# Fourier mixing and two gated layers: forward folds from GpSimd to VectorE, matrix loads ahead of folds, weight conversions at earlier steps

## The chip, the cores and the metric

The kernel runs on one core of a Trainium2 chip. The metric is the device time of one execution in microseconds (us), the median of three runs. The engines are named as in the profile: PE is TensorE (PEld its weight loads), DVE is VectorE, ACT is ScalarE, POOL is GpSimd, SP is SyncE, which only issues DMAs here.

## The reference

The input is 2 sequences of 3008 tokens with 256 features. Each is transformed along the tokens, mixed in the frequency domain by a complex 256x256 matrix with a bias, shrunk towards zero by 0.01 (soft threshold), and transformed back. The 6016 tokens then go through two gated layers of width 2048, whose weights come as 64-bit numbers; the second layer has exp(-h) in place of exp(-1.702 h).

```python
def _attn_ref(x, w_r, w_i, b_r, b_i):
    X = np.fft.rfft(x, axis=1)
    Xr, Xi = X.real, X.imag
    Yr = Xr @ w_r - Xi @ w_i + b_r
    Yi = Xr @ w_i + Xi @ w_r + b_i
    Yr = np.sign(Yr) * np.maximum(np.abs(Yr) - lam, 0.0)
    Yi = np.sign(Yi) * np.maximum(np.abs(Yi) - lam, 0.0)
    return np.fft.irfft(Y, n=x.shape[1], axis=1)

def _moe_ref(x, w_in, w_out):
    h = x @ w_in
    return (h * (1.0 / (1.0 + np.exp(-1.702 * h)))) @ w_out
```

## The kernel before

The kernel has four stages, one after another on PE.

**Forward transform** (from line 271, loop at line 458). The tokens are folded by symmetry: `fold(g)` (line 290) adds and subtracts quarter sequences on 128 partitions, so that a small matrix product does the transform. There are 16 groups, `groups`, in the order (frequency parity q, sequence b, kind t): groups 0 to 3 and 12 to 15 are q=0, groups 4 to 11 are q=1. A fold makes up to three tiles `lv` or `keep` (128x512, line 309), three tiles `xf` (128x256, line 320) and, for two kinds, two more `xf` from `dd` (line 329). The configuration strings `lv`, `dd` and `pr` say by position which engine does each: V is DVE, P is POOL. In group 2 and later, 9 operations stand on POOL: three `lv` or `keep`, four `xf` or their like at line 320 (in the groups with t=3, the ones with j=1, of which groups 13 and 15 are the last) and two at line 329. Step g of the loop issues the folds of group g+3, then `fwd_mm(g)` (line 366; matrix products at line 361), then for sequence 1 `load_m` (line 121, a DMA of a forward matrix at line 132 into one of four buffers `m0`), then `fwd_evac` of the group before (PSUM to `xt`, ACT at line 401, or ACT at line 405 and DVE at lines 391 to 417). `fold` also calls `load_raw` (line 284, a DMA at line 288 into one of three buffers). In this stage POOL and SP run in the written order; the order of DVE, ACT and PE is set at compile time by a planner with its own costs, and each engine then runs its list in that fixed order.

**Mixing** (from line 493, loop at line 567): 12 steps i of complex products (lines 518, 521), with the bias added by one product `ones` x `bias_hl` (line 524). Steps 0 and 1 use float32, the others a high and a low part `xh`, `xl`, with `wh` and `wl` (lines 502, 503). `bias_hl` is completed by a DMA on POOL (line 344). DVE and ACT threshold the result.

**Inverse transform** (from line 600): 16 steps, products at line 361 again (`psi`), evacuated by ACT and DVE, summed into `yt`, in part by accumulating DMAs on POOL (line 702).

**Two gated layers** (from line 771): per layer l, 6 blocks i of up to 1024 tokens, 8 pairs p of weight tiles. `group(l, i, p, hook)` (line 806) makes seven products (line 818) by a Strassen-like scheme, gates them on ACT (lines 821, 823), and the second products `out_mm` (line 790) follow one group later, so that group p's second weight is used in group p+1. ACT copies (lines 837, 853, 855) and DVE sums (lines 839, 863, 866) stand between the products. `hook(h)` is called at six places of a group, with h from 1 to 6. From the mixing on, every engine runs in the written order.

**Weight conversion** runs beside all this. The 32 weight tiles arrive as 64-bit numbers and become pairs of 32-bit parts. `cv_load` (line 154) loads one into `raw` (one buffer, SP, lines 162, 163, 166). `window(1, ())` (line 246) begins one conversion: `cv_bits` (line 169) has one ACT operation into `cv_c` (line 175; one buffer), then five DVE operations (lines 180 to 184) and an accumulating DMA on POOL from `cv_c` into `cv_a` (line 185), which are kept in a list that `pump` works off. `settle` hands finished ones on; `window(0, done)` places them: `place_out` (line 194: ACT at 105 and 107, a DMA on POOL at 106) or `place_in` (line 203: DVE at 213 to 216, ACT and POOL or DMAs). The order is that of `WEIGHTS` (line 33). The steps are lists in the configuration: `tf` in the forward stage (4 conversions), `tm` and `ml` in the mixing (3 conversions, and loads), `ti` in the inverse (3 conversions), `pl` in the inverse (placements), and `kb` for the 8 groups of the first block of tokens (6 conversions; at the place h=1 of the group). `pk` is how many items of the list are worked off in a step of the mixing (4).

Of the kernel before, what the change touches and what calls it, by code (L numbers as in the profile page):

```python
# [8 lines left out]

F32 = mybir.dt.float32  # L10
CFG = {'lv0': 'V', 'lv': 'VVVVVPVVVVVP', 'dd0': 'VPVVPPPPPVVP', 'dd': 'VVVVVVVVVVPV', 'ths': 'VVVVPV', 'thf': 'VVVP', 'ivf': 'V', 'cva': 'P', 'pol': 'PPPP', 'pil': 'P', 'mvl': 'PVVP', 'xl': 'V', 'xse': 'V', 'gl': 'VPPPPPPP', 'tf': [6, 9, 11, 14], 'tm': [1, 6, 10], 'ml': [4, 8], 'ti': [8, 11, 14], 'pl': [1, 4, 9, 12, 15], 'kb': [0, 1, 1, 1, 1, 1, 1, 0], 'kr': [0, 1, 0, 1, 0, 1, 1, 0], 'fa': 3, 'xp': [2, 4, 4, 5], 'xq': [1, 4, 1], 'xs': 4, 'xi': [7, 7, 9, 10, 10, 11, 8], 'xsi': 9, 'xo': (0, 1, 6, 2, 3, 4, 5), 'xd': (0, 1, 4, 6), 'ca': 4, 'tl': True, 'fwd': 'Pool,SP', 'rest0': 'all', 'rest1': 'all', 'last1': 'all', 'inv': 'all', 'mid': 'all', 'last0': 'all', 'thm': 'A', 'gl0': 'PVPVVVPV', 'gl2': 'PPPPPPPP', 'gl3': 'PPPPPPPV', 'xl0': 'V', 'xl1': 'V', 'pre': 14, 'pre2': 0, 'yd': 6, 'lvb': 6, 'mlp': 'all', 'pr': 'VVVP', 'pf': 'PV', 'eo': '0110', 'n32': 2, 'li': [8, 10, 11], 'lii': [0], 'xa': 4, 'nhb': 6, 'ddb': 6, 'mlp1': 'all', 'mlp2': 'all'}
NUM = dict(li=[5, 6, 7, 8], n32=2, pk=4, ydp=2, lii=[1, 3], xd=(), ml=[], pl=[], xo=range(7), pi=6, nhb=6, tf=[5, 9, 13], tm=[1, 3, 5, 7, 9, 11], ti=[0, 2, 4, 6, 8, 10, 12, 14, 14, 15, 15], kb=[2] * 8, kr=1, fa=3, fe=2, pm=0, nf=4, lvb=6, ddb=8, ivb=1, eob=1, fsb=6, f1=3, f2=0, fm=[7, 8, 9], fi=[1, 1, 2, 2], pre=13, pre2=1, yd=3, psh=0, ie=[12], xp=[1, 3, 4, 5], xq=[1, 2, 2], xs=5, nw=4, xi=[14, 14, 15, 15], xsi=13, rw=2, ca=4, cc=2, tb=1, tmn=1)

DEF = dict(pr="V", pf="V", lv0="V", lv="VPP", dd0="VVVVVP", dd="VPV", mpl="PV", ths="VP", thf="VVPP", fsl="VP", ivf="PPVV", cva="P", pol="P", pil="P", mvl="V", xl="PPVVPPP", xl0="PPVVPPP", xl1="PPVVPPP", xse="VP", gl="P", gl0="P", gl2="P", gl3="P", wcl="V", thc="V", thm="V")
# [7 lines left out]
P = 128  # L22
# [8 lines left out]
FS = 4  # L31

WEIGHTS = [("in", 0, p, True) for p in range(6)] + [("out", 0, p, True) for p in range(4)]
WEIGHTS += [(kind, 0, p, True) for kind, p in (("out", 4), ("out", 5), ("in", 6), ("in", 7), ("out", 6), ("out", 7))]
WEIGHTS += [(kind, 1, p, False) for kind in ("in", "out") for p in range(8)]

C_HI = float(np.uint32(0x0FEFFEF0).view(np.float32))
# [2 lines left out]
def split_sums(kind, q, p):  # L40
    return (kind, q) == ("f", 0) and CFG.get("eo", "1111")[p] == "1" or (kind, p) == ("i", 0) and CFG.get("eo", "1111")[2 + q] == "1"

# [14 lines left out]
def spectral_mlp_kernel(ctx, tc, xin, mfwd, minv, wc, bias, w_in1, w_out1, w_in2, w_out2, outT):  # L57
# [4 lines left out]
    def N(k):  # L62
        return CFG.get(k, NUM[k])

# [6 lines left out]
    def region(name):  # L71
        m = CFG.get(name, "none")
        if m == modes[-1] == "all":
# [161 lines left out]
    def settle(now=False):  # L235
        pump()
        for u, (a, c) in bits:
            if not u[3]:
                spilled[u[:3]] = d = dram_p.tile([P, 2 * CU], F32, name=f"w_{u[0]}{u[1]}_{u[2]}")
                nc.sync.dma_start(out=d, in_=a)  # L240
        fresh = [(u, a) for u, (a, _) in bits if u[3]]
        done, added[:] = (added + fresh, ()) if now else (added[:], fresh)
        bits[:] = []
        return done
# [36 lines left out]
    raws, lvs, xs = {}, {}, {}  # L281
# [174 lines left out]

    prev = None
    for g, (q, b, t) in enumerate(groups):
        fold(g + N('fa'))
        ps = fwd_mm(g)  # L460
        if b == B - 1 and m_order[0][0] == "f":
            load_m()
        if prev is not None:
            fwd_evac(*prev)
        prev = (g, ps)
        if g == 6:
            wc_p = opened("wc", "right")
            wc_s = m_p.tile([P, MW], F32, tag="m", name="wc_s")[:, : 6 * D].rearrange("p (k d) -> p k d", k=2)
            bias_hl = wc_p.tile([P, 2 * D], F32R, name="bias_hl")
            bias_lo = wc_p.tile([1, 2 * D], F32R, name="bias_lo")  # L470
            bias_f = wc_p.tile([P, 2 * D], F32, name="bias_f")
            nc.gpsimd.memset(bias_f, 0.0)
            ones = wc_p.tile([P, P], F32R, name="ones")
            ones_f = wc_p.tile([P, P], F32, name="ones_f")

            neglam = wc_p.tile([P, 1], F32, name='neglam')
            nc.vector.memset(neglam, -LAM)


        if g == 10:  # L480
            load_wc()
        if g == 13:
            prep_wc()
            lo_p.append(wc_p)
            xsplit(N('n32'), 1)
        if g == 3:
            cv_load(1)
        if g in N('tf'):
            tick(N('tf').count(g))
# [422 lines left out]
    done = []  # L912
    added.extend(hold)
    for at, (l, i, p) in enumerate(seq):
# [10 lines left out]
        def hook(h):  # L925
# [13 lines left out]
            if h == 3:  # L939
                window(0, done, True)  # L940
                done[:] = []
            if h == 1:
                window(k, ())
            if h in (2, 3):
                moved(h)
# [2 lines left out]
            if h == 4:  # L948
                pump()
                cv_load(1 - len(loaded))  # L950
            if late and (l, i, p, h) in ((0, 0, 1, 4), (0, 0, 2, 3), (0, 0, 2, 4), (0, 0, 3, 4)):
                kk, y, u, v = late.pop(0)
                (nc.vector.tensor_sub if kk in (0, 3) else nc.vector.tensor_add)(y, u, v)
# [152 lines left out]
```

## Time and profile before

| what | us |
|---|---|
| median of three runs | 1178.29 (1178.03 to 1184.57) |
| the profiled execution, its own time | 1182.72 |
| its span, first to last instruction | 1180.6 |
| PE busy | 1150.5 (97% of the span) |
| ACT / DVE / POOL busy | 773.3 / 636.1 / 502.4 |

The profile is of one execution. In its rows a time is the start in us from the begin of the span, followed by how long the merged instructions took, the engine, the line, the operation, the tiles and the count; in brackets is how long the engine had stood idle before and what ended that. Busy PE counts matrix products that are pipelined, so a product of 128x512 is shown with a longer time than the step to the next one.

### The profile page before, as it was taken

How to read it: one execution, taken by the hardware profiler on the slowest of the kernel's cores; microseconds unless marked ns; L12 is line 12 of the kernel's file. 1: busy time of each engine (PE TensorE's matmuls, PEld its weight loads, DVE VectorE, ACT ScalarE, POOL GpSimd, SP SyncE). 2: the span in 40 equal slices, each digit the busy share in tenths (PEclk: the TensorE clock that was granted, in tenths of full speed). 3: DMA queues.
4: the chain of work that ended last, by engine and by line, in shares of the span. 5: the costliest groups of instructions: out<-in, count | busy, mean ns of one | idle time of the engine just before them, and what ended most of it. 6: DMA issues, size and time to landing. Idle time of an engine off the chain costs nothing.

```text
span 1180.6 us, 14536 instructions
## 1 busy us (share of the span) xinstructions
PE 1150.5 (97%) x5052; PEld 945.3 (80%) x5052; DVE 636.1 (54%) x987; ACT 773.3 (65%) x1439; POOL 502.4 (43%) x430
## 2 busy tenths in 40 slices
PE   7889998999999999999999999999999999999998
PEld 4658885877888888888889978888888888888897
DVE  7768787776556466365564553352532623523522
ACT  2366545777668667667677787675665766766755
POOL 2355254443444444344446755433333433433333
PEclk9989999999999999999999999999999999999999
DMA  7457478432121221121130200010000000000000
GB/s 270 142 128 148 126 148 163 89 80 45 44 64 36 72 63 37 45 72 37 36 89 5 68 10 27 1 37 1 1 36 1 11 26 1 36 1 1 36 1 31
DMA packets 37835, 66.83 MB, mean 57 GB/s; under 512 B 3457, under 2 KB 14977, under 8 KB 37762
## 3 DMA queue, kind: packets, MB, share of 16 engines
q1 hardware_dynamic: 25730, 45.90, 11.9%
q0 software_dynamic: 12032, 20.01, 9.8%
q8 instruction: 39, 0.64, 0.2%
q14 instruction: 34, 0.28, 0.1%
HBM read 35.53 MB, written 10.35 MB: 39 GB/s over the span
## 4 chain that ended last, share of the span: by engine, by line
PE 76%; ACT 3%; DVE 2%; issue 1%; DMA 0%; DVEq 0%; POOL 0%; POOLq 0%
PE o L790 40%; PE x L818 36%; ACT yt L821 1%; DMA wo<-cv_a 0%; ACT x L727 0%; ACT yt L837 0%; DVE yt L839 0%; DVE tmp L213 0%; DVE yt L863 0%; ACT g L823 0%; DVE x L734 0%; ACT yt L855 0%; ACT yt L853 0%; DVE g L828 0%; DVE cv_a L182 0%
## 5 line engine op out<-in xcount | busy, mean ns | idle before, releaser
L828 POOL TENSOR_TENSOR g<-yt,g 128x512 fp32r<-128x512 f32 (+1 forms) x282 | 362.8, 1299 | 491.4 <-PE x L818 337.1
L790 PE MATMUL o<-g,wo 128*128 128x512 f32 (+1 forms) x2304 | 561.0, 386 | 2.6 <-DMA wo<-cv_a 2.6
L818 PE MATMUL x<-x,wi 128*128 128x512 f32 (+1 forms) x2016 | 501.2, 388 | 7.8 <-ACT yt L837 3.1
L790 PEld LDWEIGHTS o<-g,wo 128*128 128x128 f32 x2304 | 433.0, 188 | 83.8 <-DMA wo<-cv_a 3.1
L818 PEld LDWEIGHTS x<-x,wi 128*128 128x128 f32 x2016 | 378.2, 188 | 86.1 <-ACT yt L837 5.4
L821 ACT ACTIVATE yt<-yt 128x512 f32<-128x512 f32 (+1 forms) x288 | 179.1, 622 | 257.1 <-DVE yt L863 205.8
L823 ACT CAST g<-yt 128x512 fp32r<-128x512 f32 (+1 forms) x384 | 235.1, 612 | 12.2
L863 DVE TENSOR_TENSOR yt<-yt,x 128x512 f32<-128x512 f32 (+1 forms) x96 | 64.7, 674 | 217.2 <-PE x L818 216.7
L839 DVE TENSOR_TENSOR yt<-yt,x 128x512 f32<-128x512 f32 (+1 forms) x96 | 64.8, 675 | 167.4 <-ACT yt L837 167.4
L828 DVE TENSOR_TENSOR g<-yt,g 128x512 fp32r<-128x512 f32 (+1 forms) x102 | 70.1, 688 | 72.1 <-ACT g L823 72.1
L361 PE MATMUL psf<-m,xf 128*128 128x190 f32 (+3 forms) x224 | 57.7, 419 | 15.7 <-DVE xf L320 6.5
L361 PEld LDWEIGHTS psf<-m,xf 128*128 128x128 f32 x224 | 41.7, 204 | 31.1 <-POOL xf L320 7.9
L866 DVE TENSOR_TENSOR yt<-yt,x 128x512 f32<-128x512 f32 (+1 forms) x96 | 64.8, 675 | 0.0
L734 DVE TENSOR_TENSOR x<-yt,x 128x512 fp32r<-128x512 f32 (+1 forms) x44 | 46.1, 1047 | 29.7 <-ACT x L727 29.7
L185 POOL DMA_DIRECT2D cv_a<-cv_c x32 | 28.0, 875 | 77.5 <-DVE cv_c L184 61.4
L855 ACT COPY yt<-x 128x512 f32<-128x512 f32 (+1 forms) x96 | 55.8, 581 | 0.7 <-ACT yt L853 0.6
L821 ACT ACTIVATE yt<-x 128x512 f32<-128x512 f32 (+1 forms) x96 | 56.2, 585 | 0.0
L853 ACT COPY yt<-x 128x512 f32<-128x512 f32 (+1 forms) x96 | 55.0, 572 | 0.0
L837 ACT COPY yt<-x 128x512 f32<-128x512 f32 (+1 forms) x96 | 54.8, 571 | 0.0
L361 PE MATMUL psi<-m,f 128*128 128x376 f32 (+3 forms) x208 | 49.9, 396 | 0.0
L361 PEld LDWEIGHTS psi<-m,f 128*128 128x128 f32 x208 | 36.6, 190 | 11.9
L175 ACT ACTIVATE cv_c<-raw 128x512 f32<-128x512 f32 x32 | 21.6, 675 | 27.3 <-DMA cv_a<-cv_c 27.1
(117 smaller groups left out, 834.0 us busy)
## 6 DMA issues: line engine op xcount, KB each, us to landing
raw<-in_wi SPq DMA_DIRECT2D x32, 256.0 KB, 3.5
cv_a<-cv_c POOLq DMA_DIRECT2D x32, 256.0 KB, 5.0
raw<-in_wo SPq DMA_DIRECT2D x16, 512.0 KB, 4.0
raw<-in_x SPq DMA_DIRECT2D x12, 512.0 KB, 4.8
xl<-xt POOLq DMA_DIRECT2D x20, 256.0 KB, 5.5
out_t<-yt SPq DMA_DIRECT2D x20, 256.0 KB, 2.2
m<-in_mi SPq DMA_DIRECT2D x4, 564.0 KB, 9.1
wo<-cv_a POOLq DMA_DIRECT2D x8, 256.0 KB, 5.5
```

The source lines that it names most:

```text
L361: nc.tensor.matmul(ps, hi[:, c : c + P], m[:, k, :w], start=i == 0, stop=i == last)
L790: nc.tensor.matmul(acc[h, mm], st, mv, start=first and k == 0, stop=last and k == 2)
L818: nc.tensor.matmul(ps, st, mv, start=first and m == 0, stop=m == 2, skip_group_check=True)
L821: nc.scalar.activation(g, g if src is None else src, func)
L823: nc.scalar.copy(gh, g)
L828: eng.tensor_sub(gl, g, r32(gh))
L837: nc.scalar.copy(y1, X)
L839: nc.vector.tensor_add(y1, y1, Y)
L853: nc.scalar.copy(y2, Z)
L855: nc.scalar.copy(y3, X)
L863: nc.vector.tensor_add(y2, y2, X)
L866: nc.vector.tensor_add(y3, y3, Z)
```

## The change

- `lv`, `dd` and `pr` become 'V': all 9 fold operations of group 2 and later that stood on POOL go to DVE.
- In the loop of the forward stage, `load_m` stands before `fold`, and `fold` stands after `fwd_mm`.
- Mixing: conversions begin at steps 1, 5, 9 (were 1, 6, 10), loads at 3 and 7 (were 4 and 8), and 6 items of the list are worked off per step (were 4).
- Inverse: conversions begin at steps 5, 8, 11 (were 8, 11, 14); a sixth placement is added, at step 7.
- First block of tokens: conversions in groups 0 to 5 (were 1 to 6). In group 0 the conversion begins at h=4, its list is worked off at once and it is placed in group 1.
- The order of `WEIGHTS` has ("out", 6) before ("in", 6) and ("in", 7).

```diff
-CFG = {... 'lv': 'VVVVVPVVVVVP', 'dd': 'VVVVVVVVVVPV', 'pr': 'VVVP', 'tm': [1, 6, 10], 'ml': [4, 8], 'ti': [8, 11, 14], 'pl': [1, 4, 9, 12, 15], 'kb': [0, 1, 1, 1, 1, 1, 1, 0] ...}
+CFG = {... 'lv': 'V', 'dd': 'V', 'pr': 'V', 'tm': [1, 5, 9], 'ml': [3, 7], 'pk': 6, 'ti': [5, 8, 11], 'pl': [1, 4, 7, 9, 12, 15], 'kb': [1, 1, 1, 1, 1, 1, 0, 0] ...}
-WEIGHTS += [(kind, 0, p, True) for kind, p in (("out", 4), ("out", 5), ("in", 6), ("in", 7), ("out", 6), ("out", 7))]
+WEIGHTS += [(kind, 0, p, True) for kind, p in (("out", 4), ("out", 5), ("out", 6), ("in", 6), ("in", 7), ("out", 7))]
...
     for g, (q, b, t) in enumerate(groups):
-        fold(g + N('fa'))
         ps = fwd_mm(g)
         if b == B - 1 and m_order[0][0] == "f":
             load_m()
+        fold(g + N('fa'))
...
-            if h == 1:
+            if h == (1 if at else 4):
                 window(k, ())
...
             if h == 4:
                 pump()
                 cv_load(1 - len(loaded))
+                if at == 0:
+                    done.extend(settle(True))
```

## Rows read from the trace of the kernel before

**Rows 1.** The page: PE's busy time, and the granted TensorE clock in 40 slices
```profile
PE 1150.5 (97%) x5052; PEld 945.3 (80%) x5052; DVE 636.1 (54%) x987; ACT 773.3 (65%) x1439; POOL 502.4 (43%) x430
...
PEclk9989999999999999999999999999999999999999
```
**Rows 2.** The view of waits, engine PE, 0 to 300 us: total, times, longest
```profile
PE psf L361 <- POOL xf L320: 6.2, 3, 5.5
PE x L818 <- ACT yt L837: 3.0, 1, 3.0
PE psf L361 <- DMA m<-in_mf: 2.8, 1, 2.8
PE o L790 <- DMA wo<-cv_a: 2.6, 1, 2.6
```
**Rows 3.** The timeline of PE, from the forward transform into the mixing
```profile
28.52 2.20 PE L361 MATMUL psf<-m,xf 128*128 128x190 f32 x12 [0.49 <-DVE xf L320]
33.50 23.42 PE L361 MATMUL psf<-m,xf 128*128 128x376 f32 x98 [2.79 <-DMA m<-in_mf]
57.26 5.04 PE L361 MATMUL psf<-m,xf 128*128 128x188 f32 x30 [0.34 <-POOL xf L320]
...
68.61 4.75 PE L361 MATMUL psf<-m,xf 128*128 128x188 f32 x14 [5.49 <-POOL xf L320]
...
76.23 0.79 PE L524 MATMUL psm<-bias_hl,ones 128*128 128x512 f32 x1
```
**Rows 4.** The timelines of SP and of POOL in the forward transform
```profile
27.94 0.86 SPq L132 DMA_DIRECT2D m<-in_mf  x2
...
67.53 1.02 POOL L320 TENSOR_TENSOR xf<-keep 128x256 f32<-128x256 f32 x1
68.20 0.81 POOL L344 DMA_DIRECT2D bias_hl<-bias_lo  x1
```
**Rows 5.** The timeline of DVE at the end of the forward transform
```profile
65.93 0.69 DVE L184 SCALAR_TENSOR_TENSOR cv_c<-raw,cv_c 128x512 f32<-128x512 uint32 x1
...
67.14 0.40 DVE L320 TENSOR_TENSOR xf<-keep 128x256 f32<-128x256 f32 x1
```
**Rows 6.** The views of two tiles, DMA landing: bias_hl, then cv_c (to 300 us)
```profile
DMA to landing us min/median/max: 5.2/5.2/5.2
...
DMA to landing us min/median/max: 4.3/5.0/9.4
```
**Rows 7.** The timeline of PE, gated layers: where groups begin, and the second block
```profile
195.24 2.52 PE L818 MATMUL x<-x,wi 128*128 128x512 f32 x9
...
205.33 2.81 PE L818 MATMUL x<-x,wi 128*128 128x512 f32 x9 [0.38 <-DVE yt L863]
...
216.30 2.20 PE L818 MATMUL x<-x,wi 128*128 128x512 f32 x9
...
269.40 2.26 PE L818 MATMUL x<-x,wi 128*128 128x512 f32 x9
...
284.11 2.20 PE L818 MATMUL x<-x,wi 128*128 128x512 f32 x9
...
345.31 2.20 PE L818 MATMUL x<-x,wi 128*128 128x512 f32 x9
...
355.51 2.20 PE L818 MATMUL x<-x,wi 128*128 128x512 f32 x9
...
366.21 2.20 PE L818 MATMUL x<-x,wi 128*128 128x512 f32 x9
```
**Rows 8.** The timelines of ACT and POOL around the start of the gated layers
```profile
186.91 0.68 ACT L175 ACTIVATE cv_c<-raw 128x512 f32<-128x512 f32 x1 [3.31 <-DMA cv_a<-cv_c]
...
198.51 0.66 ACT L175 ACTIVATE cv_c<-raw 128x512 f32<-128x512 f32 x1 [5.49 <-DMA cv_a<-cv_c]
...
208.26 0.59 ACT L821 ACTIVATE yt<-x 128x512 f32<-128x512 f32 x1
...
202.30 0.86 POOL L185 DMA_DIRECT2D cv_a<-cv_c  x1 [8.03 <-DVE cv_c L184]
```

More of the change, by code (lines that the diff above doesn't have):

```diff
@@ L10 @@
 F32 = mybir.dt.float32
-CFG = {'lv0': 'V', 'lv': 'VVVVVPVVVVVP', 'dd0': 'VPVVPPPPPVVP', 'dd': 'VVVVVVVVVVPV', 'ths': 'VVVVPV', 'thf': 'VVVP', 'ivf': 'V', 'cva': 'P', 'pol': 'PPPP', 'pil': 'P', 'mvl': 'PVVP', 'xl': 'V', 'xse': 'V', 'gl': 'VPPPPPPP', 'tf': [6, 9, 11, 14], 'tm': [1, 6, 10], 'ml': [4, 8], 'ti': [8, 11, 14], 'pl': [1, 4, 9, 12, 15], 'kb': [0, 1, 1, 1, 1, 1, 1, 0], 'kr': [0, 1, 0, 1, 0, 1, 1, 0], 'fa': 3, 'xp': [2, 4, 4, 5], 'xq': [1, 4, 1], 'xs': 4, 'xi': [7, 7, 9, 10, 10, 11, 8], 'xsi': 9, 'xo': (0, 1, 6, 2, 3, 4, 5), 'xd': (0, 1, 4, 6), 'ca': 4, 'tl': True, 'fwd': 'Pool,SP', 'rest0': 'all', 'rest1': 'all', 'last1': 'all', 'inv': 'all', 'mid': 'all', 'last0': 'all', 'thm': 'A', 'gl0': 'PVPVVVPV', 'gl2': 'PPPPPPPP', 'gl3': 'PPPPPPPV', 'xl0': 'V', 'xl1': 'V', 'pre': 14, 'pre2': 0, 'yd': 6, 'lvb': 6, 'mlp': 'all', 'pr': 'VVVP', 'pf': 'PV', 'eo': '0110', 'n32': 2, 'li': [8, 10, 11], 'lii': [0], 'xa': 4, 'nhb': 6, 'ddb': 6, 'mlp1': 'all', 'mlp2': 'all'}
+CFG = {'lv0': 'V', 'lv': 'V', 'dd0': 'VPVVPPPPPVVP', 'dd': 'V', 'ths': 'VVVVPV', 'thf': 'VVVP', 'ivf': 'V', 'cva': 'P', 'pol': 'PPPP', 'pil': 'P', 'mvl': 'PVVP', 'xl': 'V', 'xse': 'V', 'gl': 'VPPPPPPP', 'tf': [6, 9, 11, 14], 'tm': [1, 5, 9], 'ml': [3, 7], 'pk': 6, 'ti': [5, 8, 11], 'pl': [1, 4, 7, 9, 12, 15], 'kb': [1, 1, 1, 1, 1, 1, 0, 0], 'kr': [0, 1, 0, 1, 0, 1, 1, 0], 'fa': 3, 'xp': [2, 4, 4, 5], 'xq': [1, 4, 1], 'xs': 4, 'xi': [7, 7, 9, 10, 10, 11, 8], 'xsi': 9, 'xo': (0, 1, 6, 2, 3, 4, 5), 'xd': (0, 1, 4, 6), 'ca': 4, 'tl': True, 'fwd': 'Pool,SP', 'rest0': 'all', 'rest1': 'all', 'last1': 'all', 'inv': 'all', 'mid': 'all', 'last0': 'all', 'thm': 'A', 'gl0': 'PVPVVVPV', 'gl2': 'PPPPPPPP', 'gl3': 'PPPPPPPV', 'xl0': 'V', 'xl1': 'V', 'pre': 14, 'pre2': 0, 'yd': 6, 'lvb': 6, 'mlp': 'all', 'pr': 'V', 'pf': 'PV', 'eo': '0110', 'n32': 2, 'li': [8, 10, 11], 'lii': [0], 'xa': 4, 'nhb': 6, 'ddb': 6, 'mlp1': 'all', 'mlp2': 'all'}
 NUM = dict(li=[5, 6, 7, 8], n32=2, pk=4, ydp=2, lii=[1, 3], xd=(), ml=[], pl=[], xo=range(7), pi=6, nhb=6, tf=[5, 9, 13], tm=[1, 3, 5, 7, 9, 11], ti=[0, 2, 4, 6, 8, 10, 12, 14, 14, 15, 15], kb=[2] * 8, kr=1, fa=3, fe=2, pm=0, nf=4, lvb=6, ddb=8, ivb=1, eob=1, fsb=6, f1=3, f2=0, fm=[7, 8, 9], fi=[1, 1, 2, 2], pre=13, pre2=1, yd=3, psh=0, ie=[12], xp=[1, 3, 4, 5], xq=[1, 2, 2], xs=5, nw=4, xi=[14, 14, 15, 15], xsi=13, rw=2, ca=4, cc=2, tb=1, tmn=1)
```

## The prediction, made before the changed kernel ran

> **What bounds the kernel now.** The page is read first. PE is busy for 1150.5 of 1180.6 us [rows 1], so at most 30 us are to be had from PE's gaps, and a little more from the clock: the granted clock falls to 8 tenths in one slice early on and to 9 in others [rows 1]. The other engines have room, so the share of busy time names PE, and the question is only where PE stands still. The view of waits of PE up to 300 us tells that [rows 2]: 6.2 us for folds on POOL, 2.8 for a forward matrix, 3.0 for an ACT copy at the start of the gated layers, 2.6 for a weight `wo` that is still in its DMA. From there on the groups begin at an even pace of 355.51 - 345.31 = 10.20 us, with 366.21 - 355.51 = 10.70 where one block of tokens follows another [rows 7], and nothing in the change touches that. So the sum is made of four places: the end of the forward transform, the mixing, the first two groups, and group 7 of the first block.
>
> **Forward transform.** Removed are three waits of PE: 2.79 at 33.50 for a matrix, 0.34 at 57.26 and 5.49 at 68.61 for a fold on POOL [rows 3]. The matrix is issued by SP at 27.94 [rows 4] because three loads of raw data stand before it in SP's queue and these wait for folds; after the change the first of the two matrices stands ahead of them and waits only for PE to leave its buffer, which is long done. Behind it SP then has the raw loads, which need folds that come later anyway, so I cost the move at nothing. A second matrix still follows the raw loads, with one group more of time. The folds: nine operations go to DVE, six of 128x256 at 0.40 and three of 128x512 at some 0.69 (taken from the nearest operation with two inputs of that size) [rows 5], 4.5 us of DVE time in 57 us; POOL took 1.02 for one [rows 4]. The one that PE waited for stood on POOL behind the DMA of the third conversion, which waits for DVE's last operation on it at 65.93 [rows 5]. In the changed kernel a fold needs nothing of the conversion, and the planner is free to put it earlier in DVE's list. I take it that it does, because there is nothing else in that list for DVE while a conversion's DMA is under way.
>
> What is late next? Without waits PE would start at 33.50 - 2.79 = 30.71, need 23.42 + 5.04 for the same products [rows 3], and 16 more of 5.04 / 30 = 0.168 each: it would end at 61.9 instead of 68.61 + 4.75 = 73.36. That is 11.5 us, of which 14 x (4.75 / 14 - 0.168) = 2.4 are the slow clock after the long wait. But the mixing cannot use all of it. Its product with `bias_hl` ran at 76.23 [rows 3]; the DMA for it was issued at 68.20 [rows 4] and takes 5.2 [rows 6], so it was there at 73.4, only 2.8 before its use. That DMA hangs on the same conversion (DVE at 65.93, then POOL). The conversion chain starts when ACT has emptied a group that PE computes after the waits of 0.49 and 2.79 [rows 3], so it moves up by about 3.3, and POOL no longer has a fold of 1.02 in front of the DMA (about 1.0). The bias is there at 73.4 - 4.3 = 69.1, and the gain is 76.23 - 69.1 = 7.1. I take 7.1 because it goes by the nearest rows. Bounds: 3.8 if the chain doesn't move (2.8 of slack and the 1.0), 11.5 if the planner finds another order for the bias; a loss has a rival of its own below.
>
> **Mixing and inverse.** The same six conversions are made, some steps sooner. PE waits for nothing there before, so I cost it at nothing. What hides it is that a step of the mixing uses two of eight PSUM banks, so PE can be some steps ahead of DVE and ACT. Were that cover gone, one conversion's DVE work, about 3 us, would show; so 0 with -1 and +3 as bounds.
>
> **Groups 0 and 1 of the gated layers.** Before, ACT stood 5.49 us until 198.51 for the release of `cv_c` [rows 8], with the copies that PE needs behind it; group 0 lasted 205.33 - 195.24 = 10.09 and group 1 216.30 - 205.33 = 10.97 [rows 7]. The conversion that blocked it is gone. But a sixth placement now stands there, of the conversion begun at step 11. The one begun at that step before ran at 186.91, and released its buffer only at 198.51 [rows 8], 3.3 after PE's 195.24. At the shortest it is 202.30 - 198.51 = 3.8 to the DMA [rows 8] and 5.0 to landing [rows 6], 8.8 in all, so 195.7. I take some 2.6 after PE's start: group 0 becomes 1.4 shorter (0.7 sooner, and ACT has one operation of 0.66 less).
>
> Then comes a wait that the change adds. Group 0 begins a conversion at h=4, group 1 begins the next at h=1. ACT has only three operations in between, of some 0.59 as the one at 208.26, after the conversion's own 0.66: 2.4 us [rows 8]. The buffer is released 8.8 after the first began. So ACT stands for 8.8 - 2.4 = 6.4 in group 1, and behind it wait the gate and both copies without which PE's fifth product cannot run; DVE's sums wait for the same, and then PE. Less some 0.6 for work that PE has in hand, PE waits 5.8, and then has the slow clock for a while, 0.7 (it lost 2.4 after 5.49 in the forward stage [rows 3], in which no product had gone before). Group 1 becomes 10.20 + 5.8 + 0.7 = 16.7, that is 5.7 longer. Both groups: +4.3. Bounds: -6.3, when ACT never waits (at most the 5.49 in group 0 and 10.97 - 10.20 in group 1), and +8.8, when it is 6.4 and 2.4 without any gain in group 0.
>
> The one price in this that decides is how long a DMA holds `cv_c`; the trace has 4.3 to 9.4 with a median of 5.0 [rows 6]. The Trainium skill, DMA: Bandwidth & Descriptors, section Anatomy of one DMA, gives a fixed part of about 2.0 us and the bytes over 436 GB/s, so by that page 256 KB would be an estimated 2.6 us, and the wait in group 1 would be 2.4 shorter, the whole sum 1169.1. Not one of the conversions in the trace shows that, and I keep 5.0.
>
> **Group 7.** Its second weight was converted in group 5, and landed late: 284.11 - 269.40 = 14.71 where 10.70 is usual [rows 7], 2.6 of it in the wait [rows 2], the rest the slow clock. After the change it is converted in group 2 and placed in group 3, and the last one is placed in group 6. So -4.0; bounds 0 and -4.0, with no reason for a loss, since groups 6 and 7 have less to do than before.
>
> **The sum.** -7.1 + 0 + 4.3 - 4.0 = -6.8. The profiled execution took 1182.72 with a span of 1180.6, so it would take 1175.9 with a span of 1173.8. It lies 4.4 above the median of the runs shown; I take the difference off the median: 1178.3 - 6.8 = 1171.5.
>
> **The rivals.**
>
> *The added wait does not come* (0.28). If the conversions in groups 0 and 1 are far enough apart, or the placement finds its data there, the two groups give -6.3 instead of +4.3, and the time is 1178.3 - 7.1 - 6.3 - 4.0 = 1160.9. For it: 5.49 us of ACT's wait are certainly at the wrong place now, and the new steps are earlier. Against it: both conversions of the inverse in the rows waited for that buffer [rows 8], and groups 0 and 1 are closer than those.
>
> *The forward stage gains little* (0.17). The conversion chain stays where it is, since its DMAs and not PE set its pace: 3.8 instead of 7.1, and 1174.8.
>
> *Slower: the folds stand behind the third conversion on DVE* (0.08). POOL's queue no longer decides, DVE's list does. If the planner puts the folds of groups 14 and 15 behind the operation at 65.93, they start at 66.6, PE starts group 14 at about 67.1 and has 32 products at the slow 0.339 [rows 3]: it ends at 77.9 instead of 73.36, +4.5. With +4.3 and -4.0 that is +4.8, and 1183.1. It decides from the point where the fold of group 14 is listed behind the third conversion.
>
> **How the numbers follow.** The forecast has 0.42, the three rivals 0.28, 0.17 and 0.08, and 0.05 is left for what I don't see, most of it a larger gain. The range is 1159.5 to 1178.5: it takes in the first two rivals and the bounds 3.8 and 11.5 of the forward stage, and leaves out the slower case and the loss of 8.8 in groups 0 and 1 together with a small gain. A measurement of this kernel can tell about 1% (11.8 us) from no change. Faster by more than that is the first rival, a tenth of the forecast and part of the rest: 0.34. Slower by more has only 0.03, since even the slower rival is within 1%. The rest, 0.63, is within 1%.
>
> **What would show it.** Right: no PE wait for `xf` on POOL or for `m` after 10 us; the first product with `bias_hl` some 7 us earlier, with its DMA just before it; in group 1 a wait of ACT at line 175 of about 6 us and PE waiting for an ACT copy at line 855; group 7 at 10.7. Wrong: the fold of group 15 still after a conversion on DVE; a group 1 of about 10 us, which is the first rival; the end of the mixing moved by less than its beginning, which would show that DVE and not PE sets the pace there; or gaps of PE in groups 2 to 6 that were not there before.

## The result, and the profile after

| | us |
|---|---|
| the kernel before, median of 6 runs | 1179.97 (1177.27 to 1184.57) |
| the changed kernel, median of 6 runs | 1193.03 (1189.46 to 1195.05) |
| ratio | 1.0102, 95% interval 1.0072 to 1.0133 |
| span of the profiled execution (its own time 1195.05) | 1193.3 |

The forecast was 1171.5 with a range to 1178.5. By the ratio the changed kernel takes some 12 us more than before (13 between the two medians), where 6.8 less were expected.

The page first, to be held against [rows 1]: PE's busy time rose by 4.6 us, and in the row of the granted clock the eighth of the 40 slices (209 to 239 us) now stands at 7 tenths.

```profile
PE 1155.1 (97%) x5052; PEld 947.8 (79%) x5052; DVE 632.6 (53%) x995; ACT 772.3 (65%) x1439; POOL 493.3 (41%) x422
...
PEclk9989999799999999999999999999999999999999
```

The view of waits, engine PE, 0 to 300 us (total, times, longest). The POOL wait of [rows 2] is gone within this stretch, and so is the weight `wo` of group 7. In their place stand waits for ACT at lines 855 and 837, for the bias, for `xl`, `wc_s` and `xh`, 21.5 us in all; before, ACT and `wo` together were 6.3 (5.6 in [rows 2], and 0.7 for line 855 further down in that view). The wait for a matrix is still there, 2.5 where it was 2.8.

```profile
PE x L818 <- ACT yt L855: 5.9, 2, 5.2
PE psm L524 <- DMA bias_hl<-bias_lo: 5.4, 1, 5.4
PE x L818 <- ACT yt L837: 4.6, 1, 4.6
PE psf L361 <- DMA m<-in_mf: 2.5, 1, 2.5
PE psm L521 <- DMA xl<-xt: 2.4, 2, 1.7
PE psm L518 <- ACT wc_s L339: 2.3, 1, 2.3
...
PE psm L521 <- ACT xh L454: 0.9, 1, 0.9
```

PE's timeline from the forward transform to the first groups (start, duration, operation, count, idle time before and its releaser), beside [rows 3] and [rows 7]:

```profile
53.05 12.05 PE L361 MATMUL psf<-m,xf 128*128 128x188 f32 x64 [2.46 <-DMA m<-in_mf]
...
67.42 3.70 PE L518 MATMUL psm<-wc_s,xt 128*128 128x512 f32 x8 [2.32 <-ACT wc_s L339]
76.57 0.77 PE L524 MATMUL psm<-bias_hl,ones 128*128 128x512 f32 x1 [5.45 <-DMA bias_hl<-bias_lo]
...
150.57 6.01 PE L361 MATMUL psi<-m,f 128*128 128x192 f32 x36
...
201.25 2.52 PE L818 MATMUL x<-x,wi 128*128 128x512 f32 x9
208.40 1.65 PE L818 MATMUL x<-x,wi 128*128 128x512 f32 x3 [4.63 <-ACT yt L837]
210.77 6.48 PE L818 MATMUL x<-x,wi 128*128 128x512 f32 x15 [0.72 <-ACT yt L855]
...
227.88 2.93 PE L818 MATMUL x<-x,wi 128*128 128x512 f32 x6 [5.15 <-ACT yt L855]
...
233.17 2.56 PE L818 MATMUL x<-x,wi 128*128 128x512 f32 x9
...
286.58 2.20 PE L818 MATMUL x<-x,wi 128*128 128x512 f32 x9
...
296.78 2.20 PE L818 MATMUL x<-x,wi 128*128 128x512 f32 x9
```

The inverse's start in the kernel before, from PE's timeline:

```profile
144.56 6.01 PE L361 MATMUL psi<-m,f 128*128 128x192 f32 x36
```

Four stages come out of the two sets of rows. The forward products now end at 53.05 + 12.05 = 65.10, where they ended at 73.36: the folds did what was asked of them. But the first product with `bias_hl` ran at 76.57 instead of 76.23, after 2.32 for `wc_s` and 5.45 for the bias. From there to the inverse it is 74.00 us, where before it was 144.56 - 76.23 = 68.33. From the start of the gated layers to group 2 it is 233.17 - 201.25 = 31.92, against 216.30 - 195.24 = 21.06 [rows 7]. And from group 2 to the second block it is 63.61, against 67.81 before, since group 7 takes 10.20 and no longer 14.71. The sum is +0.3 + 5.7 + 10.9 - 4.2 = 12.7, the difference of the spans.

The granted clock goes with the waits. The view of stretches (columns: busy time of PE, PEld, DVE, ACT and POOL with their counts, clock, DMA share, GB/s) shows a mean of 0.73 from 201 to 213 us and of 0.76 from 213 to 233, which is the level of 1.2 GHz for about half of the time and 2.4 for the rest; after 235 us it is 1.00.

```profile
213.00:233.00 20.00, 14.85 (x47) 11.43 (x46) 11.43 (x19) 10.97 (x19) 5.48 (x6) 0.76 0.32 80
```

**Where the bias was lost.** The forecast let the conversion chain move up by 3.3. Its first ACT operation moved up by 2.5, to 33.89 from 36.36; it no longer waited for PE, but now for the load of its weight. And DVE's last of five operations on it came 10.4 us after that (5.8 before), since 23 operations of folds are listed among the five, where before there were 5. The timelines of ACT and DVE, in the kernel before:

```profile
36.36 0.68 ACT L175 ACTIVATE cv_c<-raw 128x512 f32<-128x512 f32 x1
...
42.13 0.69 DVE L184 SCALAR_TENSOR_TENSOR cv_c<-raw,cv_c 128x512 f32<-128x512 uint32 x1
```

and in the changed kernel, with some of the folds of line 320:

```profile
33.89 0.68 ACT L175 ACTIVATE cv_c<-raw 128x512 f32<-128x512 f32 x1 [2.44 <-DMA raw<-in_wi]
...
39.63 1.76 DVE L320 TENSOR_TENSOR xf<-keep 128x256 f32<-128x256 f32 x5
...
44.26 0.69 DVE L184 SCALAR_TENSOR_TENSOR cv_c<-raw,cv_c 128x512 f32<-128x512 uint32 x1
```

Line 184 of the first conversion is at 44.26 instead of 42.13, and the second, third and fourth wait for one another through `cv_c`. On POOL the DMA for the bias stands behind that of the third conversion, now at 71.94 instead of 68.20 [rows 4]. It landed in 4.5, which is 76.4. POOL's timeline:

```profile
71.94 0.82 POOL L344 DMA_DIRECT2D bias_hl<-bias_lo  x1
```

The same delay reached PE in the forward stage too. SP loads the next weight into `raw` as soon as DVE has done line 184, in both kernels, and the last two forward matrices stand behind that load in SP's queue. They were issued at 45.99 (44.25 before), and PE, which came to them sooner than before, waited 2.46 at 53.05. SP's timeline:

```profile
45.42 0.47 SPq L163 DMA_DIRECT2D raw<-in_wi  x1
45.99 0.89 SPq L132 DMA_DIRECT2D m<-in_mf  x2
```

**Where the mixing lost.** The fifth conversion (the one begun at step 1 of the mixing) stands in ACT's queue and needs `cv_c` from the fourth. Before, DVE had finished the fourth at 78.49, ahead of the mixing's own sums, and ACT took the fifth at 84.17 with no wait:

```profile
84.17 0.69 ACT L175 ACTIVATE cv_c<-raw 128x512 f32<-128x512 f32 x1
```

Now the last three operations of the fourth stand between DVE's sums of step 0 (line 533), which wait for PE, and PE had waited for the bias. DVE's timeline:

```profile
82.39 0.69 DVE L533 TENSOR_TENSOR sd<-us,psm 128x512 f32<-128x512 f32 x1 [1.75 <-PE psm L518]
...
85.80 0.69 DVE L184 SCALAR_TENSOR_TENSOR cv_c<-raw,cv_c 128x512 f32<-128x512 uint32 x1
95.09 0.69 DVE L533 TENSOR_TENSOR sd<-us,psm 128x512 f32<-128x512 f32 x1 [8.60 <-ACT us L531]
```

ACT's timeline in the same stretch, the fifth conversion:

```profile
91.84 0.66 ACT L175 ACTIVATE cv_c<-raw 128x512 f32<-128x512 f32 x1 [6.74 <-DMA cv_a<-cv_c]
```

ACT stands for 6.74 us until that DMA has landed, and DVE for 8.60 behind it, because the copies of step 1 are behind the blocked operation.

PE itself lost nothing there: it was busy for all of the 14.50 us from 85.5 to 100. Of the 5.7 us, 1.5 went at the beginning, where the eight products from the first with the bias on took 5.12 us (3.63 before) at the slow clock that followed the wait (a granted clock of 0.73 from 76 to 84 us). The other 4.2 went at three stops between 129 and 141 us, where PE waited 0.88 for `xh` and 1.72 and 0.65 for `xl`; the starts of two products are 1.27, 2.11 and 1.05 apart there, where 0.23 is usual. These waits follow the five DVE operations on the conversion begun at step 5, which stand there in one piece (123.72 to 126.51) and for which ACT stood 4.54 us. conv_only, below, has the same piece, with ACT standing 4.41, and no wait of PE: there nothing had made DVE and ACT late before. The view of stretches, and PE's timeline:

```profile
85.50:100.00 14.50, 14.50 (x57) 10.53 (x56) 5.86 (x13) 5.57 (x11) 3.65 (x4) 1.00 0.43 90
100.00:150.50 50.50, 47.25 (x204) 37.85 (x203) 44.42 (x76) 31.72 (x57) 22.66 (x22) 1.00 0.71 167
```

```profile
138.52 0.50 PE L521 MATMUL psm<-wh,xl 128*128 128x512 f32 x1 [1.72 <-DMA xl<-xt]
```

**Where groups 0 and 1 lost.** ACT's timeline there, to be held against [rows 8]:

```profile
195.53 0.67 ACT L175 ACTIVATE cv_c<-raw 128x512 f32<-128x512 f32 x1 [5.94 <-DMA cv_a<-cv_c]
...
206.73 0.63 ACT L105 ACTIVATE wo<-cv_a 128x512 fp32r<-128x512 f32 x1 [5.09 <-DMA cv_a<-cv_c]
...
215.71 0.68 ACT L175 ACTIVATE cv_c<-raw 128x512 f32<-128x512 f32 x1
...
225.03 0.66 ACT L175 ACTIVATE cv_c<-raw 128x512 f32<-128x512 f32 x1 [7.02 <-DMA cv_a<-cv_c]
```

In group 0 the placement at line 105 waited 5.09 until 206.73, 5.5 behind PE's start, and the copy for PE stands behind it. The conversion that it places had begun at 195.53, 5.7 us ahead of PE's start; before, the one of that step began 8.3 ahead (186.91 [rows 8]), since it had stood only 3.31 for `cv_c`, not 5.94. In group 1 the second conversion waited 7.02 for the first one's buffer, and the copies at lines 853 and 855 stand behind that: PE's 4.63 and 5.15 above.

### The profile page after: what moved, and what is told of

It is laid out like the page before. It is cut to its first block, busy times and chain, and to the rows that moved or that the text cites. A ratio compares the mean times of both kernels' runs of the same rounds, so it can differ in the third digit from the quotient of the medians.

```text
span 1193.3 us, 14533 instructions
## 1 busy us (share of the span) xinstructions
PE 1155.1 (97%) x5052; PEld 947.8 (79%) x5052; DVE 632.6 (53%) x995; ACT 772.3 (65%) x1439; POOL 493.3 (41%) x422
## 4 chain that ended last, share of the span: by engine, by line
PE 75%; ACT 3%; DVE 2%; issue 2%; DMA 0%; POOL 0%; POOLq 0%; DVEq 0%; ACTq 0%
PE o L790 40%; PE x L818 35%; ACT yt L821 1%; DMA cv_a<-cv_c 0%; ACT x L727 0%; ACT yt L837 0%; POOL g L828 0%; ACT g L823 0%; DVE tmp L213 0%; DVE yt L839 0%; ACT yt L855 0%; DVE x L734 0%; DVE g L828 0%; ACT yt L853 0%; DVE yt L863 0%
## 5 line engine op out<-in xcount | busy, mean ns | idle before, releaser
L818 PEld LDWEIGHTS x<-x,wi 128*128 128x128 f32 x2016 | 380.4, 190 | 93.0 <-ACT yt L855 11.3
L175 ACT ACTIVATE cv_c<-raw 128x512 f32<-128x512 f32 x32 | 21.5, 671 | 35.7 <-DMA cv_a<-cv_c 33.2
```

The source lines that it names most:

```text
L818: nc.tensor.matmul(ps, st, mv, start=first and m == 0, stop=m == 2, skip_group_check=True)
```

## The experiments

Times are medians, with the ratio to the kernel before in the same batch and its 95% interval. All stage lengths are read from PE's timeline in one profile of each run: B is the first product with `bias_hl`; M runs from B to the inverse's first product; G from the gated layers' first product to that of group 2; R from there to the second block of tokens.

| run | time | ratio | B | M | G | R |
|---|---|---|---|---|---|---|
| before | | 1 | 76.23 | 68.33 | 21.06 | 67.81 |
| changed | 1193.03 | 1.0102 (1.0072 to 1.0133) | 76.57 | 74.00 | 31.92 | 63.61 |
| fwd_only | 1184.05 | 1.0020 (1.0005 to 1.0034) | 74.24 | 69.72 | 22.81 | 67.99 |
| conv_only | 1186.00 | 1.0033 (1.0015 to 1.0052) | 73.34 | 68.35 | 29.97 | 63.46 |
| no_g0 | 1190.01 | 1.0058 (1.0030 to 1.0086) | 78.86 | 73.54 | 23.24 | 67.71 |
| early_bias | 1193.24 | 1.0097 (1.0072 to 1.0121) | 70.26 | 79.37 | 30.61 | 63.53 |
| mix_old | 1192.37 | 1.0083 (1.0061 to 1.0105) | 77.00 | 69.72 | 33.38 | 63.59 |
| dve_inorder | 1187.50 | 1.0044 (1.0025 to 1.0063) | 78.35 | 69.37 | 31.67 | 63.54 |
| late_now | 1227.47 | 1.0377 (1.0355 to 1.0399) | 75.99 | 73.22 | 24.36 | 78.44 |
| no_pl15 | 1186.75 | 1.0043 (1.0026 to 1.0060) | 79.06 | 73.54 | 25.50 | 63.40 |
| best_a | 1179.09 | 0.9972 (0.9958 to 0.9987) | 75.55 | 68.34 | 21.34 | 64.12 |
| best_e | 1173.18 | 0.9927 (0.9905 to 0.9949) | 74.49 | 68.35 | 16.46 | 64.08 |
| best_f | 1179.65 | 0.9977 (0.9962 to 0.9992) | 76.58 | 71.12 | 16.18 | 64.10 |
| best_g | 1173.29 | 0.9916 (0.9899 to 0.9934) | 71.67 | 70.00 | 16.13 | 64.08 |

**fwd_only: the forward part alone.** The kernel before, with

```diff
-'lv': 'VVVVVPVVVVVP', 'dd': 'VVVVVVVVVVPV', 'pr': 'VVVP'
+'lv': 'V', 'dd': 'V', 'pr': 'V'
-        fold(g + N('fa'))
         ps = fwd_mm(g)
         if b == B - 1 and m_order[0][0] == "f":
             load_m()
+        fold(g + N('fa'))
```

> Only the forward part of the change: nine folds on VectorE, load of the matrix and the products ahead of the fold; all conversion steps as in the kernel before. Theory A (the late folds, listed among the first conversion's VectorE operations, push every later conversion back, so the bias arrives no sooner and a blocked ACT conversion stands in the mixing): the first bias product stays at 76.2 to 77, the third conversion's copy on ACT starts near 65 (was 61.2), PE waits some 2 us for wc_s and some 5 us for bias_hl, the inverse begins 4 to 7 us later than 144.56, and the time is 4 to 7 us above before. Rival R1 (the loss in the mixing comes from the conversions moved up inside the mixing): the inverse begins at 144 to 145 or sooner and the time is within 1 us of before or below it. In both the groups from the gated layers' start on are as before.

**conv_only: the moved conversions alone.** The changed kernel with those lines undone.

> Only the moved conversions (mixing, inverse, first block, order of weights); the forward part as before. Theory A: forward and mixing as before (bias product at 76.2, inverse begins within 1 us of 144.56); gated start to the start of group 2 lasts about 32 us (was 21.06), group 7 is about 4 us shorter; together 6 to 7 us above before. Rival R1: the inverse begins some 6 us later, so that the time is 12 to 13 us above before, all of the loss.

Theory A held in part at the front of fwd_only and failed behind it. The waits for `wc_s` and the bias came as expected, and ACT's block too. But the bias product came at 74.24, 2 us sooner than in the profile of before and not at 76.2 to 77, the inverse began at 143.96 and not 4 to 7 us later, and the time is 0.20% (2.4 us) above before. First PE's timeline, then ACT's line 175:

```profile
65.07 5.20 PE L518 MATMUL psm<-wc_s,xt 128*128 128x512 f32 x8 [2.75 <-ACT wc_s L339]
74.24 0.47 PE L524 MATMUL psm<-bias_hl,ones 128*128 128x512 f32 x1 [3.98 <-DMA bias_hl<-bias_lo]
...
143.96 6.01 PE L361 MATMUL psi<-m,f 128*128 128x192 f32 x36
```

```profile
89.26 0.67 ACT L175 ACTIVATE cv_c<-raw 128x512 f32<-128x512 f32 x1 [6.60 <-DMA cv_a<-cv_c]
```

Rival R1 failed as well: in conv_only the mixing took 68.35, as before, and the time is 0.33% (3.9 us) above it, less than the 6 to 7 expected, with G at 29.97. Either half alone leaves M at 68 to 70, both together make it 74. Neither theory has a place for that, so a third was formed: the two halves use up the same lead of PE, once. In M the two together cost 4.3 us more than the two alone added up (5.7 against 1.4 and 0.0). The 1.4 of fwd_only is the slow clock behind the wait for the bias (0.79 from 74 to 82 us): from 82 to 144 us PE was busy there without a gap, although ACT was blocked as in the changed kernel. Group 1 and group 7 went with the conversions, as both theories had it. Group 0 did not quite: in fwd_only G is 1.8 longer than before. ACT's conversion of step 11 had to wait there for the load of its weight, until 188.00, so that the next one got `cv_c` at 199.21, 4.6 us after PE's start and not 3.3, and PE waited 4.3 for the copy behind it and not 3.0. The ratios tell the same: 0.20% and 0.33% alone, 1.02% together; the 0.5% between is some 6 us, uncertain by 4 to 5.

**no_g0: no conversion in group 0.** The changed kernel with the conversions in groups 1 to 6 and the old order of the weights.

```diff
-'kb': [1, 1, 1, 1, 1, 1, 0, 0]
+'kb': [0, 1, 1, 1, 1, 1, 1, 0]
```

> The changed kernel without its conversion in group 0: conversions in groups 1 to 6 again and the old order of the weights; the sixth placement in the inverse at step 7 and steps 5, 8, 11 stay. Theory B (two conversions share cv_c within 12 us, so ACT blocks in group 1, and PE's slow clock after it doubles the loss): group 1 back to 10.2 to 11.5 us, gated start to group 2 some 24 to 27 us, group 7 again 14 to 15 us, time 2 to 5 us under the changed kernel. Rival R2 (the placement at step 15 alone, by which ACT waits 5 us in group 0, makes the loss): gated start to group 2 stays at 31 to 32 us, and the time is 4 us above the changed kernel by group 7.

G fell from 31.92 to 23.24 and group 7 was long again, 294.03 - 279.40 = 14.63. So the conversion in group 0 costs 8.7 us, and late_now, below, shows that it is its distance to the next one. Rival R2 falls as the whole cause. The placement's share stayed: PE waited 4.58 at the start of group 0, as before 4.63.

**early_bias: the mixing weights prepared sooner.**

```diff
-        if g == 10:
+        if g == 7:
             load_wc()
-        if g == 13:
+        if g == 9:
             prep_wc()
```

> The changed kernel with the load of the mixing weights at step 7 (was 10) and their preparation, with it the DMA of bias_hl, at step 9 (was 13), ahead of the third conversion. Theory A: the waits of 2.3 for wc_s and 5.4 for bias_hl are gone, the first bias product runs at 68 to 70, and if ACT's blocked conversion in the mixing were the whole rest, the inverse begins 4 to 8 us before 150.57; time 4 to 8 us under the changed kernel. If the fourth conversion's late end alone sets the pace of the mixing (rival A2), the inverse begins within 1.5 us of 150.57 though the bias came sooner, and the time is within 2 us of the changed kernel.

The bias product ran at 70.26 with no wait, 6.3 sooner, and the inverse began only 0.9 sooner, at 149.63. The time is that of the changed kernel. This is rival A2: ACT's conversions in the mixing waited for `cv_c` longer than in the changed kernel (4.58 and 8.27, there 1.14 and 6.74), and PE's waits moved from the bias to `xh`. ACT's timeline and PE's waits from 60 to 155 us:

```profile
91.55 0.66 ACT L175 ACTIVATE cv_c<-raw 128x512 f32<-128x512 f32 x1 [8.27 <-DMA cv_a<-cv_c]
```

```profile
PE psm L521 <- ACT xh L454: 5.9, 3, 4.2
```

So the step of the forecast that led from the bias to the gain was wrong twice. The bias did not move, and where it does, with the mixing's new steps, DVE and ACT set the pace behind it.

**mix_old: the mixing's old steps in the changed kernel.**

```diff
-'tm': [1, 5, 9], 'ml': [3, 7], 'pk': 6
+'tm': [1, 6, 10], 'ml': [4, 8], 'pk': 4
```

> The changed kernel with the mixing's conversions at the old steps (1, 6, 10, loads at 4 and 8, four items of the list per step). After the first four runs theory A alone no longer does: the folds alone and the moved conversions alone leave the mixing (first bias product to the inverse's start) at 69.7 and 68.4 us, both together make it 74.0. Theory I (interaction: the late fourth conversion has used up PE's lead, and the steps 5 and 9 with six items at a time then find none): the mixing takes 69 to 70.5 us, the inverse begins at 145.5 to 147.5, PE's waits for xl and xh (3.3 us) are gone, and the time is 3 to 5 us under the changed kernel. Rival (ACT's blocked fourth conversion alone makes the loss): the mixing stays at 73 to 75 us and the time within 1 us of the changed kernel.

M is 69.72 and the waits for `xl` and `xh` are gone: theory I, in the size expected. ACT's block at step 1 is still there (6.72), and PE was busy without a gap from 84 to 147 us, so the block alone costs PE nothing; the 1.4 over before are the slow clock behind the wait for the bias (0.79 from 76 to 84 us). The run puts back three settings at once, the steps, the loads and the items per step, and does not tell which of them counts. Of the 4.3 us only some 2 reached the time (1.0083 against 1.0102, with overlapping intervals). In the profile G grew to 33.38: PE came to the gated layers 3.7 us sooner, but the conversion that is placed in group 0 began only 2.2 sooner (193.31), so PE waited 6.0 instead of 4.6 for the copy behind the placement.

**dve_inorder: DVE in written order.** In the changed kernel the planner no longer orders DVE in the forward stage.

```diff
-'fwd': 'Pool,SP'
+'fwd': 'Pool,SP,DVE'
```

> The changed kernel with VectorE in written order in the forward stage too, so that no late fold stands among the operations of the first conversion. Theory A (those folds make every later conversion late): VectorE's last operation of the first conversion is done within 7 us of the conversion's ACT operation (10.4 now), the fourth conversion's ACT operation comes 4 us or more sooner than 91.84, the inverse begins at 144 to 147, and the time is 4 to 6 us under the changed kernel. Rival (the planner's order is still the better one, since folds now stand behind conversions that wait for DMAs): PE waits for folds on VectorE for 3 us or more in all after 10 us, and the forward transform ends after 68; the time is that of the changed kernel or above.

"Fourth conversion's ACT operation" names the one at 91.84, which is the fifth and waits for the fourth's DMA. DVE's five operations on the first conversion were at their last 5.0 us after ACT's (10.4 in the changed kernel), the fourth was finished before the mixing's sums (its last operation at 82.82, the first sum at 87.18), and ACT took the fifth at 89.18 with no wait, 2.7 sooner and not 4. M is 69.37 although the mixing has the new, early steps. That is the other half of theory I: take away the late fourth conversion, and steps 5 and 9 cost 1.0 us. ACT's timeline:

```profile
89.18 0.66 ACT L175 ACTIVATE cv_c<-raw 128x512 f32<-128x512 f32 x1
```

The rival has its share: behind the first fold PE waited 4.7 us for others on DVE (none in the changed kernel), and then 4.9 for `wc_s`, so that B was 78.35 and the inverse began at 147.72, above the expected 144 to 147. The time is 1.0044, some 7 us under the changed kernel, more than the 2.85 by which the inverse began sooner in the profile; the profiled execution (1191.83) was the slowest of the run.

**late_now: a whole group between two conversions.**

```diff
-            if h == (1 if at else 4):
+            if h == 4:
                 window(k, ())
...
-                if at == 0:
-                    done.extend(settle(True))
+                done.extend(settle(True))
```

> The changed kernel with every conversion of the first block begun at place h=4 of its group, as in group 0, and handed on at once: two conversions are then a whole group (10.2 us) apart instead of 5. Theory B (two conversions closer together than the 8.8 us for which cv_c is held): ACT's wait of 7.0 for cv_a in group 1 falls below 2, PE's 5.2 there goes with the slow clock behind it, the gated layers' start to group 2 lasts 23 to 26 us (31.9), and the time is 6 to 8 us under the changed kernel. Rival (the wait moves on: a conversion that is placed 8.7 us after its beginning finds its data not landed): PE waits 1 to 3 us in each of groups 1 to 6, and the time is within 2 us of the changed kernel.

Both were right about the waits, each about its place, and neither about the time. G fell to 24.36, as theory B has it, with two conversions still there, so it is their distance that cost group 1. Then R grew by 14.8: a weight that is placed this soon after its conversion is not there yet (ACT stood 1.27 and 1.35 us for it in groups 2 and 3), and groups 2 to 7 last 14.9, 11.3, 14.0, 14.2, 12.3 and 11.7 us. The edit reached further than its expectation says, since the line serves the second layer's 16 conversions too. From the second block on the span grew by another 27 us, with 18 waits of PE (view of waits, PE, 303 to 1226 us):

```profile
PE x L818 <- ACT yt L855: 19.5, 18, 2.2
```

So in this kernel the short distance between two conversions can't be mended by moving all of them to a later place.

**no_pl15: without the placement at step 15 of the inverse.**

```diff
-'pl': [1, 4, 7, 9, 12, 15]
+'pl': [1, 4, 7, 9, 12]
```

> The changed kernel without the placement at the inverse's step 15; the weight is placed with the others in group 0's window instead. Theory: ACT's wait of 5.1 for cv_a before group 0's copies goes, and with it PE's 4.6 for a copy at line 837 and 1 to 2 us of slow clock; the gated start to group 2 is 4 to 6 us shorter than 31.9, and the time 4 to 6 us under the changed kernel. Rival (the placement only changes its place: it still stands ahead of group 0's later copies on ACT, which wait for the same DMA or for the DVE sums): 0 to 1.5 us.

The wait at line 837 fell from 4.6 to 0.3 and G from 31.92 to 25.50, a little more than expected. Group 1 kept its wait (6.10, where it was 5.15). It can be read by itself in PE's timeline here:

```profile
209.01 2.37 PE L818 MATMUL x<-x,wi 128*128 128x512 f32 x9 [0.15 <-DVE yt L863]
...
223.51 2.93 PE L818 MATMUL x<-x,wi 128*128 128x512 f32 x6 [6.10 <-ACT yt L855]
...
228.79 2.32 PE L818 MATMUL x<-x,wi 128*128 128x512 f32 x9
```

Group 1 takes 19.78, in best_e below 10.40: 9.4 more, of which 6.4 are waits (6.10, and 0.28 for a copy) and 3.0 the slow clock behind them.

**best_a: group 7 alone.** The kernel before, with its finished weight of group 6 placed two places sooner.

```diff
-            if h == 3:
+            if h == (1 if at == 6 else 3):
                 window(0, done, True)
```

> The kernel before with one line changed: in group 6 of the first block the finished weight is placed at place h=1 instead of h=3, some 5 us sooner. It is the one whose DMA lands 2.6 us too late for group 7. Theory G7 (only that landing makes group 7 long): group 7 lasts 10.2 to 10.7 us instead of 14.71 and nothing else changes, time 3.5 to 4.3 us under before. Rival (the landing moves with the queue and not with the issue, or the placement blocks ACT): group 7 stays above 12 us or group 6 becomes longer by as much, and the time is within 1 us of before.

Group 7 took 280.03 - 269.31 = 10.72, so the late landing was all of it. The time fell by 3.25 us, a little less than expected, because the next group, at 280.03, lasted 10.97: a smaller wait for the next `wo` moved there (0.47 at 283.16). PE's timeline:

```profile
269.31 2.20 PE L818 MATMUL x<-x,wi 128*128 128x512 f32 x9
...
280.03 2.20 PE L818 MATMUL x<-x,wi 128*128 128x512 f32 x9
```

**best_e: and nothing in ACT's way at the start of group 0.**

```diff
-'ti': [8, 11, 14], 'pl': [1, 4, 9, 12, 15]
+'ti': [5, 8, 11], 'pl': [1, 4, 7, 9, 12]
```

> The run before it, plus the inverse's conversions at steps 5, 8, 11 and the placements at 1, 4, 7, 9, 12, so that none stands at step 15. Theory P (the placement at step 15 makes PE's wait at the start of group 0): PE's 3.0 for a copy at line 837 is gone, the gated layers' start to group 2 lasts 20.4 to 21 us, and the time is 0.5 to 2.5 us under the run before it. Rival (some other operation stands there as soon): 21 us or more, no difference in time.

PE's wait at line 837 is gone, as theory P has it, but its price was underestimated: G is 16.46 and not 20.4 to 21, and the time is 5.9 us under best_a. Group 0 has no second products (line 790) in it and lasts 6.06 if nothing waits. I had taken 10.20 for the shortest group. PE's timeline:

```profile
193.52 3.53 PE L818 MATMUL x<-x,wi 128*128 128x512 f32 x12
...
199.58 2.37 PE L818 MATMUL x<-x,wi 128*128 128x512 f32 x9 [0.16 <-DVE yt L863]
...
209.98 2.20 PE L818 MATMUL x<-x,wi 128*128 128x512 f32 x9
```

So before held 21.06 - 16.46 = 4.6 us of such losses itself; the changed kernel's two (6.4 by no_pl15, 8.7 by no_g0) stand on that floor: 16.46 + 6.4 + 8.7 = 31.6, and 31.92 was measured. This is the best version with the forward stage untouched: 1173.18, 0.9927 of before.

**best_f and best_g: the folds again, on top of best_e.** Both have the lines of fwd_only and of early_bias. best_f adds DVE in written order; best_g has the planner's order and the mixing's conversions at steps 2, 6, 10.

> The second of these, plus the forward part of the change with VectorE in written order and the mixing weights prepared at step 9. Theory A with I (the folds on VectorE cost nothing if they stand behind the first conversion, the bias is early, and the mixing keeps the old steps): forward ends at 65 to 67, first bias product at 68 to 71, mixing 69 to 70 us, inverse at 138 to 141, and the time is 3 to 6 us under the second run, that is 7 to 11 under before. Rival (VectorE's backlog and not PE sets the pace of the mixing, as in the run with the early bias alone): inverse at 143 to 146 in spite of the early bias, time that of the second run.

> As the third, but with the planner's own order of VectorE, and the mixing's first conversion at step 2 instead of 1, behind the fourth conversion's DMA. Theory: ACT's blocked operation in the mixing (8.3 with the early bias alone) is below 2.5, bias product at 69 to 71, mixing 69 to 72, inverse at 139 to 142, time 2 to 5 us under the second run. Rival (VectorE's backlog): inverse at 143 to 147, no gain.

In best_f PE waited 17.3 us in the forward stage for folds on DVE (7.7 in best_e, with 4.5 for POOL), B was 76.58, and the time is 6.5 us above best_e: worse than its own rival. In best_g the inverse began at 141.67, as the theory has it. The bias product came 0.7 too late for its range, at 71.67, and ACT's blocked operation in the mixing waited 4.14 and not below 2.5. The time is that of best_e (0.9916 against 0.9927, with overlapping intervals). The inverse took 195.75 - 141.67 = 54.08 where it took 50.7 to 50.8 in all runs before these two, and PE waited in it for ACT (1.1 for `eo`, line 648) and DVE (0.6 for `rt`, line 391), where in best_e it had no wait.

What PE won in the forward stage was given back one stage later. That the cause is the work of DVE and ACT, which was not less, is read from these waits and was not tested.

## Why the prediction was wrong, point by point

**Forward, -7.1 forecast, +0.3 in the two profiles.** That PE's wait for POOL would go is right, and the end of the products came out 8.3 sooner, of the 11.5 that the forecast had. The wait for a matrix did not go, it moved from 33.50 to 53.05 (2.46, for the last two matrices). The move was costed at nothing, and what stands ahead of those two in SP's queue, the load that waits for the first conversion, was not looked at. The step that failed is "the conversion chain ... moves up by about 3.3". Its beginning moved up by 2.5, its end came 2 to 4 later, because the planner did just what the forecast assumed: it put the folds early in DVE's list. I took DVE to be idle there. It was in the middle of the first conversion, and the conversion, not the fold, led to the bias. The rival on DVE's list looked for folds behind the third conversion and not for conversions behind folds.

Four profiles have the forward stage of before instruction for instruction (before, conv_only, best_a, best_e), with B at 73.34 to 76.23; six have that of the changed kernel (changed, fwd_only, no_g0, mix_old, late_now, no_pl15), with 74.24 to 79.06. The means are 74.9 and 77.0. So the forward part gains nothing and may lose 2 us, and the profile of before, on which my 7.1 was built, was the slowest of its four.

**Mixing, 0 forecast with a bound of +3, +5.7 in the profiles.** The named cover, "PE can be some steps ahead of DVE and ACT", exists: in fwd_only and in conv_only PE has no wait in the mixing behind the first bias product. What failed is costing the two parts apart. They draw on one cover. That it is this cover is read from the place of PE's waits, at 129 to 141 us, behind ACT's block and the conversion of step 5; how many steps PE was ahead was not measured. I had put down, as a sign of this, that the end of the mixing would move by less than its beginning. It came 6.0 later, its beginning 0.3.

**Groups 0 and 1, +4.3 forecast, +10.9 measured.** The mechanism was right in both halves: a placement in ACT's way in group 0, and a second conversion that waits for `cv_c` in group 1 with the copies behind it. The wait of ACT there was 7.02 against the forecast 6.4, PE's 5.15 against 5.8. Two terms were mis-sized. The placement came 5.5 after PE's start, not 2.6: the forecast took over the place of the conversion of step 11 from before, and in the changed kernel that conversion itself waited longer for `cv_c` (5.94, 3.31 before) and began later against PE. So group 0 became longer by some 2 us (31.92 less the 19.8 that group 1 takes in no_pl15 leaves 12.1, against 10.09) and not shorter by 1.4. And the slow clock in group 1 cost 3.0 in no_pl15, not 0.7, and more in the changed kernel, where group 1 began still at that clock (15 products in 6.48 us from 210.77, where 9 take 2.20 at the full clock): my 0.7 was a guess set below the 2.4 of the forward stage, with no row of its own. The hold of `cv_c` in group 1 was 9.3, from 215.71 to 225.03, where the forecast had 8.8, and the DMA in it about as long as the trace of before had it (4.9 in the middle up to 300 us, from issue to landing, 5.0 in [rows 6]). The estimate of 2.6 us by the Trainium skill, DMA: Bandwidth & Descriptors, section Anatomy of one DMA, would have made the term smaller still; no run shows it (the shortest of these DMAs took 3.3 us in each run's whole trace), and the measurement sides with the trace.

**Group 7, -4.0 forecast, -4.2 measured from group 2 to the second block.** Right, and best_a shows that the landing of one weight was the whole of it.

**The rivals.** The first, no added wait, needed conversions further apart than they are. The second is nearest to what became of the forward stage, but its 3.8 was still a gain. The slower one had the right engine and the wrong victim. None had a loss in the mixing, since I had taken it for safe.

**What stays open.** fwd_only has both the folds on DVE and the new order of `load_m`, `fwd_mm` and `fold`; which of the two made the planner list 23 operations of folds among the first conversion was not separated. It was not tried to keep the folds on DVE and bar the planner from listing them inside a conversion while it orders the rest.

## What to carry to other kernels

Work that is taken off one in-order engine lands in the list of another: before counting its duration, look at what the new engine has in hand at that moment and who waits for the end of that, here a chain of conversions that share one buffer. Two parts of a change that are each hidden by the same lead must be costed together, and an engine that waits must be looked up by what stands behind the waiting instruction, since 7 us of ACT's wait for one buffer cost PE nothing by themselves in the mixing, and in group 1 5 to 6 us and then 3 more at the slow clock. The cheapest gain was already in the profile of before: the wait at the start of group 0 and the weight that landed late, 9 us of 1182 in best_e without a fold moved.

## What the runs showed of the hardware that was not expected

The same instruction lists, run again, differ up to the bias by 2.9 us (B 73.34 to 76.23 in four profiles) and by 4.8 (74.24 to 79.06 in six; fwd_only and no_g0, of the same batch, by 4.6), while M agrees within 0.02 us over the four with the old forward part (68.33 to 68.35). The one wait for a fold on POOL was 5.49 in the profile that the forecast used and 3.16 in conv_only, whose forward instructions are the same. A term taken from that stage of a single profile carries an error of that size. PE's timeline of conv_only, beside the row at 68.61 of [rows 3]:

```profile
66.29 3.71 PE L361 MATMUL psf<-m,xf 128*128 128x188 f32 x14 [3.16 <-POOL xf L320]
```
